# Splitting two feed-forward steps by head pair, and scoring two tiles in one task, in a planned attention and feed-forward kernel

## The chip, the cores and the metric

The kernel runs on one core of one Trainium2 chip. The metric is the device time of one execution in microseconds (us). Three runs of the kernel before gave 613.16, 611.17 and 612.41 us, so the median is 612.41 us. Names used below: PE is TensorE, PEld its weight loads, DVE is VectorE, ACT is ScalarE, POOL is GpSimd, SP is SyncE, whose queue issues nearly all DMAs.

## The reference

Attention over 4 batches, 8 heads, 768 positions of 64 features, in which a query sees the first 4 positions (sinks) and the last 128 positions up to itself; its output, as 3072 tokens of 512 features, goes through a feed-forward layer of width 2048 with an ELU.

```python
scores = scale * q @ k.T                    # scale = 1/8
keep = is_sink | ((rel >= 0) & (rel < window))
a = softmax(where(keep, scores, -1e9))      # per head
x = (a @ v) as [3072, 512]
h = x @ w_in                                # 512 -> 2048
g = where(h > 0, h, exp(min(h, 0)) - 1)
out = g @ w_out                             # 2048 -> 512
```

## The kernel before

**Tiles and chunks.** The 24 query tiles of 128 tokens are cut into nine chunks (CHUNKS). Chunks 0 and 1 hold two tiles each, all of them first tiles of a batch, whose scores are 128 columns wide. Chunk 2 holds two second tiles (260 columns), the others three tiles. Each chunk goes through four head pairs, then through sixteen feed-forward steps f of 128 hidden features; chunks 0 and 1 interleave theirs (PARTS): steps 0 to 6 of chunk 0, 0 to 12 of chunk 1, then the rest of each.

**Attention of one tile and pair, in chunks 0 and 1.** PE makes the scores of both heads from the f32 tile `kqs` (a ring of two, loaded by SP, L568) into banks `s0` and `s1` (L668). DVE adds the mask and takes the row minimum (L683), ACT takes the exponential and its sum (L688), ACT or POOL (L692) and DVE (L697) make the reciprocal. Chunk 0 then turns the result on PE: POOL scales an identity (L704, `pq`), PE multiplies (L710, into `acc`), ACT or DVE copies out (L714, `pt`), and PE multiplies by the values (L727, into `po`). From chunk 1 on ACT and DVE split the result into two f16 parts (L742, L743), SP transposes by DMA (L761), and PE multiplies by f16 parts of the values (L775). At the end of a pair ACT and DVE write the f16 parts of x (L817, L818).

**A feed-forward step.** PE makes h from the x of all four pairs and one weight piece in twelve products (L845), ACT the exponential (L854), POOL or DVE and then DVE the ELU (L856, L857), ACT and POOL its two f16 parts (L859, L866), and PE adds six or more products into `acc` (L873). h has two banks, so step f + 2 waits for L857 of step f. Each of the 32 weight pieces is loaded by SP (L354, `raw`) and unpacked by ACT (L347), DVE (L348), ACT (L507, high part) and POOL (L508, low part in two halves).

**What sets the order.** All of this is written as tasks with an assumed duration, their dependences and rings of buffers. A planner (class Plan) lays them out in time once, and every engine's instructions are issued in that order; an engine never passes a waiting instruction. For PE, `pos` gives a task's place within its line (scores, values, transposes, feed-forward are four lines), and a line's tasks are never swapped. SHIFTS holds seeds of random shifts of due times that the plan went through. Where the plan has a gap on PE in its first 100 us, `with_idle_products` puts in unread products of 240 columns of constants (L446), filling the share IDLE_FILL of it: 0.65, or 0.75 in the first 8 us.

Of the kernel before, what the change touches and what calls it, by code (L numbers as in the profile page):

```python
# [21 lines left out]
P = 128  # L22
B, H, S, D = 4, 8, 768, 64
# [3 lines left out]
ND = DM // P  # L27
# [3 lines left out]
KW = NS + P  # L31
# [18 lines left out]
ROUNDS = 8  # L50
SHIFTS = [600047, 600054, 600066, 600067, 600150, 600157, 600163, 600185, 600194, 600295, 600400, 600467, 600483, 600849, 601310, 601684, 602239, 602260, 603167, 603862]
VISIT = 2
PAIRS = 3
LATE = 1.0
SPARE = 0.1
KEEP = 1
DUP = 3
# [4 lines left out]
FIRST, IDLE_US, IDLE_UNTIL, IDLE_LEAST, IDLE_OVER, IDLE_WANT = (13, 2), 0.11, 100.0, 0.3, 3.4, 0.85  # L62
IDLE_FILL, IDLE_FIRST = (0.65, 0.75), 8.0
V_AT = 7
V_AT0 = 5.0
T_AT = 3.5
PE_T, PE_V = 0.25, 0.13
# [45 lines left out]
class Plan:  # L113
# [7 lines left out]
    def add(self, eng, dur, fn, *args, deps=(), lat=0.0, pos=None, or_=None, line=0, slow=1.0, lock=True):  # L121

        t = Task(eng, dur, fn, args, deps, lat, pos, slow)
        t.line = line
        t.lock = lock
        if or_:
            t.ways[or_[0]] = or_[1:]
        self.tasks.append(t)
        return t

    def ring(self, name, writers, users):

        r = self.rings.setdefault(name, [])
        r.append((writers, users))
# [268 lines left out]
def fast_path(tc, ctx, first, kq, vx, wt, out, low, spread, copied, numbers, flag):  # L403

    nc = tc.nc
# [30 lines left out]
    w = rows("w", [P, 2, 512], F16, NW)  # L436
# [29 lines left out]
    add, ring = plan.add, plan.ring  # L466
# [50 lines left out]
    base, pos = {}, 0  # L517
# [29 lines left out]
    def attention(c):  # L547
# [80 lines left out]
        for p in range(NP):  # L628
# [6 lines left out]
            for g in ts:  # L635
# [34 lines left out]

                if c >= DUP:
                    scs = [add("PE", 0.222 if nb == 2 else 0.2, scores([e]), deps=kqp[e][2:4], pos=at[k] + 0.01 * e, line=1) for e in range(2)]
                else:
                    scs = [add("PE", 0.7 if nb == 2 else 0.45, scores([0, 1]), deps=kqp[0][2:4], pos=at[k], line=1)] * 2
                for kk, sc_ in zip(kqp, scs):
                    kk[4].append(sc_)
                if c < DUP and j == 0:
# [3 lines left out]
                for e in range(2):  # L681
                    ee, me = e3[:, e, :wd], mn[:, e : e + 1]
                    red = add("DVE", 0.08 + 0.00103 * wd, lambda ee=ee, me=me, sp=sps[e], m=m, wd=wd, to_score=to_score: nc.vector.tensor_tensor_reduce(ee, sp[:, :wd], m[:, :wd], to_score, 3.0e38, ALU.add, ALU.min, me), deps=[scs[e], (None, second_)[t] if t < 2 else rest_])  # L683
                    ring(f"s{banks_of[e]}", [scs[e]], [red])
# [140 lines left out]
    def feed_forward(c, f0, f1, start):  # L825
# [7 lines left out]
        for f in range(f0, f1):  # L833
# [13 lines left out]

            s1 = add("PE", 12 * (n / 2400 + 0.002), stage1, deps=[v for d in x for v in d[2:4]] + list(w_done[2 * f]), pos=start + 2 * (f - f0))
            for d in x:
                d[4].append(s1)  # L850

# [5 lines left out]
            b = last_g[0] = add("DVE", dve_us(n), lambda gf=gf, hp=hp: nc.vector.scalar_tensor_tensor(gf, gf, 0.0, hp[:, :n], ALU.min, ALU.max), deps=[b])  # L857
            ring("h", [s1], [b])
            th = add("ACT", act_us(n), lambda gf=gf, gh=gh: nc.scalar.activation(gh[:, :n], gf, AF.Copy), deps=[b])  # L859
# [425 lines left out]
```

## Time and profile before

| | |
|---|---|
| median of three runs | 612.41 us |
| the profiled execution's own time | 615.44 us |
| its span, first to last instruction | 613.6 us |
| PE busy | 605.5 us (99%) |
| DVE, ACT, POOL busy | 480.7, 428.8, 307.2 us |
| last product of the last feed-forward step ends | near 608.7 us |
| first product of a feed-forward step (chunk 0) | 31.70 us |
| first product of chunk 1's feed-forward | 56.44 us |

The span is 1.84 us shorter than the profiled execution's own time. PE busy includes unread products, so a busy PE is no proof of useful work in the first 56 us. Instruction times in the rows overlap their neighbours by about a tenth of a microsecond, since an instruction starts before the one ahead of it has drained.

### The profile page before, as it was taken

To read this page: it belongs to the slowest core of one execution; us is meant where nothing else is said; L and a number is where in the kernel's file an instruction comes from. 1 tells how busy PE (TensorE), PEld (TensorE's weight loads), DVE (VectorE), ACT (ScalarE), POOL (GpSimd) and SP (SyncE) were. 2 spreads that over 40 slices of the span, in tenths; PEclk is the share of its full clock that TensorE was granted. 3 is DMA by queue.
4 is the path that set the end of the run, shared out by engine and by line. 5 is a ranking of instruction groups with operands and counts; after the bars stand their busy time and mean duration, and the time that the engine had idled before them with its cause. 6 is when DMAs were issued, how large, how long until landed. Compare 5 with 4: busy or idle time off the path is not lost.

```text
span 613.6 us, 13574 instructions
## 1 busy us (share of the span) xinstructions
PE 605.5 (99%) x4590; PEld 368.9 (60%) x4590; DVE 480.7 (78%) x1211; ACT 428.8 (70%) x1202; POOL 307.2 (50%) x587
## 2 busy tenths in 40 slices
PE   9899999999999999999999999999999999999996
PEld 6665666667765555656565565655656565556663
DVE  5798989799898568899799988799988977543333
ACT  6899999789888567786677766677766766422222
POOL 4766899646555343353454554345554544222221
PEclk9799999999999999999999999999999999999999
DMA  8899987879797545596678945699774893524201
GB/s 295 282 252 246 336 235 247 188 171 198 170 170 204 107 98 105 153 262 138 151 174 251 232 129 142 135 256 217 147 185 102 226 165 73 110 75 109 62 1 56
DMA packets 125999, 105.22 MB, mean 171 GB/s; under 512 B 100580, under 2 KB 100836, under 8 KB 125924
## 3 DMA queue, kind: packets, MB, share of 16 engines
q1 hardware_dynamic: 125780, 104.17, 67.9%
q8 instruction: 37, 0.61, 0.4%
q14 instruction: 38, 0.31, 0.2%
q10 hardware_dynamic: 144, 0.13, 0.1%
HBM read 72.82 MB, written 7.34 MB: 131 GB/s over the span
## 4 chain that ended last, share of the span: by engine, by line
PE 96%; DVE 1%; DMA 1%; issue 0%; ACT 0%
PE h L845 41%; PE acc L873 40%; PE po L775 3%; PE s L662 3%; PE s L663 3%; PE s L775 2%; PE s L668 2%; PE acc L446 1%; DMA kqs<-in_kq_dram 1%; PE po L873 1%; PE acc L710 0%; DVE wv L348 0%; PE s L780 0%; PE po L780 0%; DVE e L683 0%
## 5 line engine op out<-in xcount | busy, mean ns | idle before, releaser
L845 PE MATMUL h<-x,w 128*128 128x384 f16 (+1 forms) x1728 | 273.6, 308 | 0.0
L845 PEld LDWEIGHTS <-w 128*128 128x128 f16 x1728 | 168.3, 98 | 84.2 <-ACT g L854 0.3
L866 POOL TENSOR_TENSOR gl<-g,gh 128x384 f16<-128x384 f32 (+1 forms) x144 | 129.5, 900 | 140.6 <-ACT gh L859 132.4
L873 PE MATMUL acc<-w,gh 128*128 128x512 f16 (+1 forms) x768 | 190.3, 375 | 0.0
L873 PEld LDWEIGHTS <-gh 128*128 128x128 f16 x800 | 76.9, 98 | 65.5 <-ACT g L854 1.4
L854 ACT ACTIVATE g<-h 128x384 f32<-128x384 f32 (+1 forms) x144 | 64.6, 449 | 67.6 <-PE h L845 65.2
L688 ACT ACTIVATE e<-e,st 128x260 f32<-128x260 f32 (+1 forms) x192 | 93.1, 485 | 26.6 <-DVE st L683 24.4
L743 DVE SCALAR_TENSOR_TENSOR pq<-e,st,pq 128x256 f16<-128x256 f32 (+1 forms) x176 | 100.0, 588 | 14.6 <-ACT pq L742 13.9
L873 PE MATMUL acc<-w,gl 128*128 128x512 f16 (+1 forms) x384 | 107.8, 375 | 0.0
L859 ACT ACTIVATE gh<-g 128x384 f16<-128x384 f32 (+1 forms) x144 | 69.3, 482 | 54.0 <-DVE g L857 53.4
L683 DVE CUSTOM_DVE_ANT_0 e<-s,m 128x260 f32<-128x260 f32 (+1 forms) x192 | 75.4, 398 | 22.6 <-PE s L663 18.3
L742 ACT ACTIVATE pq<-e,st 128x256 f16<-128x256 f32 (+1 forms) x176 | 79.5, 488 | 13.1 <-DVE st L697 12.5
L857 DVE SCALAR_TENSOR_TENSOR g<-g,h 128x384 f32<-128x384 f32 (+1 forms) x144 | 72.3, 503 | 13.0 <-POOL g L856 11.7
L856 POOL TENSOR_SCALAR g<-g 128x384 f32<-128x384 f32 (+1 forms) x77 | 41.5, 539 | 64.2 <-ACT g L854 63.4
L856 DVE TENSOR_SCALAR g<-g 128x384 f32<-128x384 f32 (+1 forms) x67 | 27.8, 415 | 50.8 <-ACT g L854 50.1
L873 PEld LDWEIGHTS <-gl 128*128 128x128 f16 x400 | 39.1, 98 | 44.2 <-POOL gl L866 0.5
L577 ACT ACTIVATE kq<-kqs 128x912 f16<-128x912 f32 (+1 forms) x48 | 48.5, 1010 | 8.6 <-PE s L663 6.0
L508 POOL TENSOR_TENSOR w<-wv,w 128x256 f16<-128x256 f32 x64 | 52.4, 838 | 3.0 <-ACT w L507 2.3
L692 POOL TENSOR_SCALAR st<-st 128x2 f32<-128x2 f32 x83 | 24.7, 298 | 48.4 <-ACT e L688 43.3
L578 DVE SCALAR_TENSOR_TENSOR kq<-kqs,kq 128x528 f16<-128x528 f32 (+1 forms) x48 | 39.3, 818 | 2.6 <-ACT kq L577 2.1
L662 PE MATMUL s<-kq 128*128 128x260 f16 x144 | 39.5, 275 | 0.0
L663 PE MATMUL s<-kq 128*128 128x260 f16 x144 | 39.5, 274 | 0.0
(105 smaller groups left out, 676.9 us busy)
## 6 DMA issues: line engine op xcount, KB each, us to landing
raw<-in_wt_dram SPq DMA_DIRECT2D x32, 512.0 KB, 5.2
kqs<-in_kq_dram SPq DMA_DIRECT2D x24, 522.0 KB, 3.9
kqs<-in_kq_dram SPq DMA_DIRECT2D x24, 456.0 KB, 3.9
vs<-in_vx_dram SPq DMA_DIRECT2D x34, 256.0 KB, 3.5
vm<-in_kq_dram SPq DMA_DIRECT2D x24, 261.0 KB, 4.2
out_dram<-wv SPq DMA_DIRECT2D x23, 256.0 KB, 2.5
vm<-in_kq_dram SPq DMA_DIRECT2D x24, 228.0 KB, 4.2
vm<-in_vx_dram SPq DMA_DIRECT2D x9, 512.0 KB, 5.1
```

Source lines behind the costliest of these rows:

```text
L662: nc.tensor.matmul(sp[:, :wd], q, hi[:, c0 : c0 + wd], start=True, stop=False)
L683: red = add("DVE", 0.08 + 0.00103 * wd, lambda ee=ee, me=me, sp=sps[e], m=m, wd=wd, to_score=to_score: nc.vector.tensor_tensor_reduce(ee, ...
L688: ex = add("ACT", 0.278 + 0.00083 * wd, lambda ee=ee, me=me, rs=rs[:, e : e + 1]: nc.scalar.activation(ee, ee, AF.Exp, bias=me, scale=-1.0 ...
L742: a = add("ACT", act_us(nb * P, True), lambda src=src, hi=hi, re=re: nc.scalar.activation(hi, src, AF.Copy, scale=re), deps=[rr])
L743: b = add("DVE", 0.45 if nb == 2 else 0.3, lambda src=src, hi=hi, lo=lo, re=re: nc.vector.scalar_tensor_tensor(lo, src, re, hi, ALU.mult, ...
L845: nc.tensor.matmul(hp[:, :n], win[:, part, d, :], xx[:, :n], start=k == 0, stop=k == 3 * ND - 1)
L854: a = add("ACT", 0.13 + 0.00091 * n, lambda gf=gf, hp=hp, sums=sums: nc.scalar.activation(gf, hp[:, :n], AF.Exp, scale=1.0 / G_SCALE, accu ...
L856: b = add("DVE", 0.06 + 0.00057 * n, lambda gf=gf: nc.vector.tensor_scalar(gf, gf, -1.0, G_SCALE, ALU.add, ALU.mult), deps=[a], slow=2.1, ...
L857: b = last_g[0] = add("DVE", dve_us(n), lambda gf=gf, hp=hp: nc.vector.scalar_tensor_tensor(gf, gf, 0.0, hp[:, :n], ALU.min, ALU.max), dep ...
L859: th = add("ACT", act_us(n), lambda gf=gf, gh=gh: nc.scalar.activation(gh[:, :n], gf, AF.Copy), deps=[b])
L866: tls.append(add("POOL", pool_us(cut), lambda gl=gl, gf=gf, gh=gh, cut=cut: nc.gpsimd.tensor_tensor(gl[:, :cut], gf[:, :cut], gh[:, :cut], ...
L873: nc.tensor.matmul(bank[:, cs], gg[:, i * P : (i + 1) * P], wout[:, part, cs], start=f == f0 and k == 0, stop=f == f1 - 1 and k == 2)
```

## The change

Four edits act together, and all of them change only the first part of the program in what is computed when; the seeds are new, so the plan of the whole program is another one.

1. TWIN: in chunks 0 and 1 the scores of both tiles of a pair are one PE task of four products, with tile j in columns 128 j of the two score banks. The banks are free for the next pair when all four DVE reductions are done.
2. SPLIT: steps 0 and 1 of chunk 0 make h in four pieces of three products, one for each head pair, each depending on that pair's x and the weight piece alone. The last piece keeps the old place.
3. IDLE_FILL: unread products fill 0.85 of a planned gap in place of 0.65 (0.75 in the first 8 us as before). The program has 94 of them, before 75.
4. SHIFTS: 34 other seeds in place of 20.

```diff
-SHIFTS = [600047, 600054, ...
+SHIFTS = [1010003, 1010007, ...
+SPLIT = 2
+TWIN = (0,1,)
-IDLE_FILL, IDLE_FIRST = (0.65, 0.75), 8.0
+IDLE_FILL, IDLE_FIRST = (0.85, 0.75), 8.0
+SPLIT_AT = -8.0
...
+                if c in TWIN:
+                    sps = [s_ps[e][:, j * P : (j + 1) * P] for e in range(2)]
+                    if j == 0:
+                        def scores_of_all(qo=qo, c0=c0, kqp=kqp):
+                            for i in range(nt):
+                                for e in range(2):
+                                    r = slice(e * D, (e + 1) * D)
+                                    nc.tensor.matmul(s_ps[e][:, i * P : (i + 1) * P], ...)
+                        scs = [add("PE", 0.23 * nt + 0.2, scores_of_all, deps=kqp[0][2:4], pos=at[k], line=1)] * 2
+                        taken = [[], []]
+                        for e in range(2):
+                            ring(f"s{e}", scs[:1], taken[e])
...
+            def of_one(d, hp=hp, f=f):
+                win = w[2 * f].rearrange("p t (a f) -> p t a f", a=ND)
+                xh, xl = x[d][:2]
+                for k, (part, xx) in enumerate(((0, xh), (1, xh), (0, xl))):
+                    nc.tensor.matmul(hp[:, :n], win[:, part, d, :], xx[:, :n], ...)
+            if c == 0 and f < SPLIT:
+                ahead = [add("PE", 3 * (n / 2400 + 0.002), of_one, d, deps=list(x[d][2:4]) + list(w_done[2 * f]), pos=...) for d in range(ND)]
```

Line numbers move by 3 to 33. The places of the lines named here in the changed program: scores L682 (128 columns) and L671 (260), pieces of h L873, whole h L866, transposes L731, values L748, unread products L449, loads of kqs L571, of vs L595, of weight pieces L357, second products L906.

**SP's queue, the first loads.** `kqs_63` and `kqs_64` are the two buffers of the kqs ring, so their loads in turn are pairs 2 and 3 of chunk 0, then pairs 0 and 1 of chunk 1; `raw` is a weight piece, `vs_66` the values of the second tile. Before:

```order
L592 DMA vs_66<-in_vx_dram 128x512
L354 DMA raw<-in_wt_dram 128x2048 x4
L568 DMA kqs_63<-in_kq_dram 128x520
L354 DMA raw<-in_wt_dram 128x2048
L568 DMA kqs_64<-in_kq_dram 128x520
L354 DMA raw<-in_wt_dram 128x2048 x3
L568 DMA kqs_63<-in_kq_dram 128x520
L354 DMA raw<-in_wt_dram 128x2048 x2
L568 DMA kqs_64<-in_kq_dram 128x520
```

and in the changed program:

```order
L357 DMA raw<-in_wt_dram 128x2048
L595 DMA vs_66<-in_vx_dram 128x512
L357 DMA raw<-in_wt_dram 128x2048
L571 DMA kqs_63<-in_kq_dram 128x520
L357 DMA raw<-in_wt_dram 128x2048 x3
L571 DMA kqs_64<-in_kq_dram 128x520
L357 DMA raw<-in_wt_dram 128x2048
L571 DMA kqs_63<-in_kq_dram 128x520
L357 DMA raw<-in_wt_dram 128x2048
L571 DMA kqs_64<-in_kq_dram 128x520
```

The first pair of chunk 1 now has six weight pieces ahead of it (before eight), the second seven (before ten), and the first weight piece goes ahead of vs_66.

**PE's queue, from the third tile's transposes of chunk 0 on.** `acc` is written by transposes, `po` by values, `s` by scores, `h_165` is the h bank of step 0 and `w_133` its weights. Before:

```order
L710 MATMUL acc_169<-pq_108,e_99 128x128 x2
L727 MATMUL po_172<-pt_110,vs_66 64x128 x2
...
L710 MATMUL acc_170<-pq_106,e_97 128x128 x2
...
L727 MATMUL po_172<-pt_111,vs_65 64x128 x2
L668 MATMUL s_167<-kqs_63 128x128
L668 MATMUL s_168<-kqs_63 128x128
L727 MATMUL po_172<-pt_112,vs_66 64x128 x2
```

and in the changed program:

```order
L731 MATMUL acc_169<-pq_108,e_99 128x128 x2
L682 MATMUL s_167<-kqs_63 128x128
L682 MATMUL s_168<-kqs_63 128x128
...
L748 MATMUL po_172<-pt_111,vs_65 64x128 x2
L873 LDWEIGHTS w_133
L873 MATMUL h_165<-x,w_133 128x256
...
L731 MATMUL acc_170<-pq_106,e_97 128x128 x2
...
L748 MATMUL po_172<-pt_112,vs_66 64x128 x2
```

The scores of pair 2 (`kqs_63`, both tiles) went ahead of the last transposes of pair 1, and the first piece of step 0 now stands ahead of those transposes too.

**PE's queue, at the first product of chunk 1's feed-forward** (`h_166<-x,w_133`). `s<-kqs 128x260` are scores of chunk 2, `pt_112,vh_80` the last values of chunk 1. Before:

```order
L668 MATMUL s_167<-kqs_64 128x260
L668 MATMUL s_168<-kqs_64 128x260
L845 LDWEIGHTS w_133
L845 MATMUL h_166<-x,w_133 128x256
```

and in the changed program:

```order
L796 MATMUL po_172<-pt_112,vh_80 64x128
L671 MATMUL s_167<-kqs_63 128x260
L671 MATMUL s_168<-kqs_63 128x260
L449 LDWEIGHTS const-bfloat16-1.0
L449 MATMUL acc_171<-const-bfloat16-1.0 128x240
L866 LDWEIGHTS w_133
L866 MATMUL h_166<-x,w_133 128x256
```

Before, four score tasks of chunk 2 stand ahead of this product (the last one of kqs_64); now there are five (the last one is the next pair's, kqs_63). All else that stands ahead of it, unread products aside, is equal in number: 84 products of h, 30 second products, and the scores, transposes and values of chunks 0 and 1.

## Rows read from the trace of the kernel before

**Rows 1.** Busy us by engine and stage, granted TensorE clock (PEclk), DMA.

```profile
core 0: us, PE busy (x) PEld busy (x) DVE busy (x) ACT busy (x) POOL busy (x), PEclk, DMA share, GB/s
24.00:32.00 8.00, 7.95 (x48) 6.04 (x49) 5.12 (x21) 6.26 (x20) 5.24 (x7) 0.60 0.87 309
32.00:56.40 24.40, 23.94 (x202) 14.98 (x200) 21.58 (x77) 24.40 (x89) 18.83 (x34) 1.00 0.94 218
56.40:608.70 552.30, 552.28 (x4208) 333.46 (x4207) 437.83 (x1045) 380.00 (x1040) 268.73 (x510) 1.00 0.67 163
```

**Rows 2.** The chain that ended last, 0 to 64 us: start, us, what.

```profile
17.16 0.71 PE s L668 x3
17.88 6.03 DMA kqs<-in_kq_dram
24.05 0.80 PE s L668 x4
24.85 2.00 PE acc L710 x8
26.85 0.62 PE po L727 x4
28.92 0.87 PE acc L710 x4
31.86 1.31 PE h L845 x12
56.51 1.42 PE h L845 x12
```

**Rows 3.** ACT in order of time: start, us, what [idle before <-releaser].

```profile
5.67 0.40 ACT L688 ACTIVATE e<-e,st 128x128 f32<-128x128 f32 x1 [3.33 <-DVE st L683]
26.76 0.40 ACT L688 ACTIVATE e<-e,st 128x128 f32<-128x128 f32 x1 [1.19 <-DVE st L697]
30.86 0.38 ACT L817 ACTIVATE x<-po 128x256 f16<-128x256 f32 x1 [0.28 <-PE po L727]
55.62 0.36 ACT L817 ACTIVATE x<-po 128x256 f16<-128x256 f32 x1
```

**Rows 4.** ACT by line, 0 to 56.4 us: count, busy us, mean ns, idle before.

```profile
L688 ACT ACTIVATE e<-e,st 128x128 f32<-128x128 f32 (+1 forms) x36 | 14.5, 404 | 5.9 <-DVE st L683 4.7 <-DVE st L697 1.2
L347 ACT ACTIVATE wu<-raw 128x512 f16<-128x512 bf16 x14 | 10.8, 770 | 0.0
L507 ACT ACTIVATE w<-wv 128x512 f16<-128x512 f32 x14 | 8.6, 621 | 0.7 <-DVE wv L348 0.7
L742 ACT ACTIVATE pq<-e,st 128x128 f16<-128x128 f32 (+1 forms) x17 | 6.0, 398 | 0.0
L817 ACT ACTIVATE x<-po 128x256 f16<-128x256 f32 x8 | 2.9, 368 | 0.5 <-PE po L727 0.5
```

**Rows 5.** PE in order of time, as rows 3.

```profile
4.38 0.80 PE L668 MATMUL s<-kqs 64*128 64x128 f32 x4
10.52 0.71 PE L710 MATMUL acc<-pq,e 128*128 128x128 f32 x4
15.43 0.49 PE L668 MATMUL s<-kqs 64*128 64x128 f32 x4
24.05 0.80 PE L668 MATMUL s<-kqs 64*128 64x128 f32 x4 [0.66 <-DMA kqs<-in_kq_dram]
35.36 1.48 PE L845 MATMUL h<-x,w 128*128 128x256 f16 x12
48.48 0.71 PE L668 MATMUL s<-kqs 64*128 64x260 f32 x4
53.04 0.59 PE L446 MATMUL acc<-const-bfloat16-1.0 128*128 128x240 bf16 x4
```

**Rows 6.** SP's queue, 0 to 70 us: waited for, us in total, times, longest.

```profile
SPq L568 <- PE s L668: 12.0, 5, 4.3
```

**Rows 7.** POOL in order of time, as rows 3: low halves of the first weight pieces.

```profile
13.46 1.75 POOL L508 TENSOR_TENSOR w<-wv,w 128x256 f16<-128x256 f32 x2
15.53 4.28 POOL L508 TENSOR_TENSOR w<-wv,w 128x256 f16<-128x256 f32 x5 [0.32 <-ACT w L507]
```

More of the change, by code (lines that the diff above doesn't have):

```diff
@@ L50 @@
 ROUNDS = 8
-SHIFTS = [600047, 600054, 600066, 600067, 600150, 600157, 600163, 600185, 600194, 600295, 600400, 600467, 600483, 600849, 601310, 601684, 602239, 602260, 603167, 603862]
+SHIFTS = [1010003, 1010007, 1010026, 1010053, 1010059, 1010083, 1010114, 1010156, 1010214, 1010335, 1010370, 1010388, 1010446, 1010468, 1010520, 1010534, 1010619, 1010737, 1010767, 1010772, 1010927, 1011110, 1011137, 1011191, 1011408, 1011660, 1012947, 1012951, 1013013, 1013279, 1013732, 1013934, 1013984, 1014001]
 VISIT = 2
+SPLIT = 2
+TWIN = (0,1,)
 PAIRS = 3
@@ L669, in scores @@
                     return run
-                if c >= DUP:
+                if c in TWIN:
[5 more added lines that the diff above has]
+                                    r = slice(e * D, (e + 1) * D)
+                                    nc.tensor.matmul(s_ps[e][:, i * P : (i + 1) * P], kqp[0][0][r, qo + i * P : qo + (i + 1) * P], kqp[0][0][r, c0 + i * KW : c0 + i * KW + P], start=True, stop=True)
+                        scs = [add("PE", 0.23 * nt + 0.2, scores_of_all, deps=kqp[0][2:4], pos=at[k], line=1)] * 2
+                        taken = [[], []]
+                        for e in range(2):
+                            ring(f"s{e}", scs[:1], taken[e])
+                elif c >= DUP:
                     scs = [add("PE", 0.222 if nb == 2 else 0.2, scores([e]), deps=kqp[e][2:4], pos=at[k] + 0.01 * e, line=1) for e in range(2)]
@@ L675, in attention @@
                 for kk, sc_ in zip(kqp, scs):
-                    kk[4].append(sc_)
+                    if c not in TWIN or j == 0:
+                        kk[4].append(sc_)
                 if c < DUP and j == 0:
@@ L683, in attention @@
                     red = add("DVE", 0.08 + 0.00103 * wd, lambda ee=ee, me=me, sp=sps[e], m=m, wd=wd, to_score=to_score: nc.vector.tensor_tensor_reduce(ee, sp[:, :wd], m[:, :wd], to_score, 3.0e38, ALU.add, ALU.min, me), deps=[scs[e], (None, second_)[t] if t < 2 else rest_])
-                    ring(f"s{banks_of[e]}", [scs[e]], [red])
+                    if c in TWIN:
+                        taken[e].append(red)
+                    else:
+                        ring(f"s{banks_of[e]}", [scs[e]], [red])
                     red.spare = SPARE if c >= PAIRS else 0.0
@@ L846, in stage1 @@
                         k += 1
-            s1 = add("PE", 12 * (n / 2400 + 0.002), stage1, deps=[v for d in x for v in d[2:4]] + list(w_done[2 * f]), pos=start + 2 * (f - f0))
-            for d in x:
-                d[4].append(s1)
+            def of_one(d, hp=hp, f=f):
+                win = w[2 * f].rearrange("p t (a f) -> p t a f", a=ND)
+                xh, xl = x[d][:2]
+                for k, (part, xx) in enumerate(((0, xh), (1, xh), (0, xl))):
+                    nc.tensor.matmul(hp[:, :n], win[:, part, d, :], xx[:, :n], start=d + k == 0, stop=d == ND - 1 and k == 2)
+            if c == 0 and f < SPLIT:
+                ahead = [add("PE", 3 * (n / 2400 + 0.002), of_one, d, deps=list(x[d][2:4]) + list(w_done[2 * f]), pos=start + 2 * f if d == ND - 1 else SPLIT_AT + 2.4 * d + 0.01 * f) for d in range(ND)]
+                for d, s1 in zip(x, ahead):
+                    d[4].append(s1)
+                h_first = ahead[0]
+            else:
+                h_first = s1 = add("PE", 12 * (n / 2400 + 0.002), stage1, deps=[v for d in x for v in d[2:4]] + list(w_done[2 * f]), pos=start + 2 * (f - f0))
+                for d in x:
+                    d[4].append(s1)
             at = (c * NF + f + 1) % nc1
@@ L857, in feed_forward @@
             b = last_g[0] = add("DVE", dve_us(n), lambda gf=gf, hp=hp: nc.vector.scalar_tensor_tensor(gf, gf, 0.0, hp[:, :n], ALU.min, ALU.max), deps=[b])
-            ring("h", [s1], [b])
+            ring("h", [h_first], [b])
             th = add("ACT", act_us(n), lambda gf=gf, gh=gh: nc.scalar.activation(gh[:, :n], gf, AF.Copy), deps=[b])
```

## The prediction

> **What bounds the kernel now.** I read the busy times by stage first, then the chain of waits, then PE's and ACT's instructions in order of time, and last what SP's queue waits for. The stages show that from 56.4 to 608.7 us PE is busy for 552.28 of 552.30 us [rows 1]; the span ends 4.9 us later. Nothing in that stretch waits on PE, so the end is fixed by two things: when the first product of chunk 1's feed-forward starts (56.44, on the chain at 56.51 [rows 2]), and how much PE work is still behind it. What the change does before that point counts only as far as it moves these two.
>
> In the 24.4 us before it ACT is busy for 24.40 us, PE for 23.94 [rows 1]. Both look full, but the product at 56.51 needs the x of chunk 1's last pair, which ACT starts to write at 55.62 [rows 3]; until then ACT has no idle time since 30.86. So ACT decides: the end of the stage is the time at which ACT comes to that instruction, which is its work ahead of it plus its idle time since its first exponential at 5.67 [rows 3]. That idle time is 5.9 - 3.33 = 2.6 us ahead of exponentials, 0.7 ahead of L507 and 0.5 ahead of L817, 3.8 us in all [rows 3, 4], and it lies before 31 us. The largest single gap, 1.19 us, ends at 26.76 [rows 3]. The chain says where it comes from: the scores at 17.16 release a kqs buffer, its load takes from 17.88 to 23.9, PE waits 0.66 us for it at 24.05, and two tiles' transposes stand behind these scores in PE's queue [rows 2, 5]. From there the granted clock is low (0.60 in the mean of 24 to 32 us [rows 1], so mostly the level of 1.2 GHz).
>
> **The change part by part.**
>
> *Scores of two tiles in one task.* The number of products is the same. It moves the second tile's scores up to the first's. SP waited 12.0 us in five waits for scores before it could issue a load of kqs [rows 6]; these waits shrink. For the load at 17.88: the first tile's scores of that pair ended near 15.9 (15.43 + 0.49), the second tile's would end 0.4 later, near 16.3, so the load starts at least 1.5 us earlier and, with the same 6.03 us, lands near 22.4, ahead of 24.05. That the order puts two fewer weight pieces ahead of it is not counted. The 0.66 us wait goes. The cost: DVE's first reduction now reads the bank that is written last, so it waits for four products in place of two: 0.73 us later at the start, where four rows take 0.80 less their overlap [rows 5]. This is idle time of ACT at its first exponential; it is in the sum below as a part of what ACT does not win.
>
> *Clock after 24 us.* The chain's pieces there are long: scores 0.80 where the same take 0.49 at 15.43, eight transposes 2.00 where two groups of four take 0.71 each, four more transposes 0.87 against 0.71 [rows 2, 5]. That is 0.31 + 0.58 + 0.16, about 1.1 us, with the values' 0.62 perhaps 1.3. In the changed order PE has 24 products of h and more unread products in that stretch and no wait for a load, so I take it at the full level. Together: 0.66 + 1.1 = 1.8 us for ACT's x of chunk 0's last pair (30.86) at the least. The most is ACT's whole idle time less the later start, 3.8 - 0.7 = 3.1. I take 2.3, nearer to the end that rests on rows.
>
> *ACT's own queue.* Counting the two orders up to that x: the changed one has two L347 and two L507 fewer ahead of it (1.54 + 1.24 us), two L742, one exponential with its sum and one L714 more; net about 1.3 us less. Up to the x of chunk 1's last pair the two orders differ by 0.1 us of work only. So 1.3 us of weight work that before was done ahead of 30.86 now stands between the two, in the stage where ACT has no gap: 2.3 - 1.3 = 1.0 us is left. The x comes at 54.6 in place of 55.62. Bounds: no gain at all if ACT's gaps only move (0), and 3.1 - 0.1 = 3.0 us.
>
> *Steps 0 and 1 by head pair.* 24 products of 256 columns, 2.6 us at 1.31 for twelve [rows 2], move into PE's early gaps; 18 of them stand ahead of the last x. This frees PE by up to 2.6 us at step 2 (35.36 [rows 5]). I cost it at nothing in the sum: what is late next is step 0's exponential and ELU (step 2 needs its bank), and then ACT's x of chunk 1; PE would only wait there. If PE were the bound, the 2.6 us would count in full.
>
> *Unread products.* 19 more, at about 0.13 us by the four that take 0.59 at 53.04 [rows 5]. Groups of 14 now stand before step 2 of chunk 0 and between two score tasks of chunk 2. They lie where PE waits for ACT and cost nothing; without that cover a group of 14 costs up to 1.8 us.
>
> *One more score task of chunk 2 ahead of the point that counts.* Five in place of four, by the order; one row of it takes 0.71 less an overlap [rows 5], 0.65 us. This work is taken out of the stretch without gaps and done where PE waits for ACT. That is a gain of 0.65 whatever else happens, unless its load is late.
>
> *The rest of the plan.* After the point the kinds of work and their neighbours on PE are the same in number, so the 552.3 us stay, less the 0.65.
>
> Sum: 1.0 + 0.65 = 1.65 us off the span of 613.6, so 611.95; the profiled execution's own 615.44 would be 613.8. The runs shown have a median of 612.41, 3.0 below that execution; I put the same difference on them: 610.8 us.
>
> **The rivals.**
>
> *B, PE's lead survives.* ACT's gaps all go and the new order feeds it without a break. Then the x comes 3.0 us earlier, and with 0.65 the time is 612.41 - 3.65 = 608.8. For it: the kqs loads come up to several us earlier, and 3.8 us of idle are there to be had. Against it: ACT starts 0.7 later, and 4.7 - 3.33 = 1.4 us of its idle time come from DVE's reductions [rows 4], which now wait for more products than before.
>
> *C, slower: the pieces of step 0 and 1 block PE's queue.* The first piece stands ahead of the transposes of pair 1's second tile, and the pieces of step 1 ahead of pair 3's scores. Each needs a whole weight piece. Before, POOL ended the first one's low halves at 15.2 and the second one's near 17.2 [rows 7], and PE needed neither until 31.86 [rows 2]. If POOL is not earlier, PE waits about 1.7 us twice, everything of chunk 0 behind it is 3.4 us late, and the slow clock stays as it was: the gain of 2.3 is not made, the x of chunk 1 comes at 55.62 + 3.4 + 0.1, the time is 612.41 + 3.5 - 0.65 = 615.3. It decides once the two waits together exceed about 2 us. For it: POOL's first halves now stand behind three scaled identities. Against it: SP loads the first weight piece before vs_66 now, and before, PE came to that place with unread products to spare. The Trainium skill, "TensorE: Matmul & The Clock Gate", Part 2, step-by-step, says that matmuls stay in program order and only weight loads are pulled ahead; by that rule any late weight is paid by all transposes behind it, as in this rival. The trace agrees: at 24.05 PE waited 0.66 us for a load with eight transposes behind it [rows 5].
>
> *D, nothing comes through.* ACT's gaps move but stay, and the fifth score task waits for its load, which in the order stands behind one of the transposes of chunk 1's last pair. Then the point is at 56.4 as before and the time between 611.8 and 613.0. For it: every us of this stage was ACT's already.
>
> **How the numbers follow.** Forecast 0.52, with 609.9 to 611.9 as its own range; B 0.16; C 0.12; D 0.20. A difference of 0.3% is 1.84 us, about what a measurement of this kernel can tell from none. Below 610.57 lie B and half of the forecast's case: 0.16 + 0.26 = 0.42 for faster. The other half and D give 0.46 for the same, C gives 0.12 for slower. The range from 608.8 to 613.0 leaves out most of C and the far end of B.
>
> **What would show it.** Right: no wait for kqs near 24 us and a granted clock of 1.00 from about 10 us on; the load of chunk 1's first pair issued by 16.5; x of chunk 0's last pair near 28.6 on ACT and of chunk 1's near 54.6; PE waiting or in unread products for one to two us ahead of that; 551.6 us without a gap behind it. Wrong: any PE wait after 60 us (then the new seeds, not the early edits, set the time); PE waiting for w before 18 us (C); the first product of chunk 1 at 53.5 or earlier (B).

## The result and the profile after

The changed kernel takes 615.61 us (median of 8 runs, 614.79 to 618.75), the kernel before 611.96 (8 runs, 611.17 to 613.19): a ratio of 1.0053, 95% interval 1.0035 to 1.0072. Timed again beside 26 runs of the kernel before it took 615.09 against 612.11, a ratio of 1.0039 (1.0021 to 1.0057). So the change costs 2.4 to 3.2 us by the two ratios. Forecast were 610.8 us, with a range up to 613.0: the sign is wrong, and the time is outside the range.

The profiled execution took 615.83 us with a span of 613.9. Its busy times by stage (as [rows 1]; the stages are cut at ACT's x of the last pair of chunk 0 and of chunk 1, and at the first product of chunk 1's feed-forward):

```profile
core 0: us, PE busy (x) PEld busy (x) DVE busy (x) ACT busy (x) POOL busy (x), PEclk, DMA share, GB/s
0.00:29.61 29.61, 25.57 (x190) 18.32 (x190) 19.86 (x94) 21.20 (x71) 17.00 (x43) 0.88 0.78 261
29.61:56.66 27.05, 24.54 (x216) 16.18 (x213) 24.95 (x80) 26.20 (x90) 19.82 (x33) 1.00 1.09 265
57.31:609.00 551.69, 551.66 (x4204) 333.12 (x4202) 432.57 (x1038) 381.75 (x1044) 270.40 (x510) 1.00 0.68 162
```

The third row is as forecast: PE has no gap, and the stretch is 0.6 us shorter than the 552.3 of [rows 1]. All that is lost is lost ahead of it. In the second row ACT is busy for 26.20 of 27.05 us, where the kernel before needed 24.76 for the same stage (30.86 to 55.62 in [rows 3]). ACT's gaps in order of time, and the two x:

```profile
5.47 0.40 ACT L709 ACTIVATE e<-e,st 128x128 f32<-128x128 f32 x1 [3.12 <-DVE st L701]
9.33 0.40 ACT L709 ACTIVATE e<-e,st 128x128 f32<-128x128 f32 x1 [1.98 <-DVE st L701]
11.82 0.39 ACT L735 ACTIVATE pt<-acc 128x256 f32<-128x256 f32 x1 [0.89 <-PE acc L731]
29.61 0.36 ACT L838 ACTIVATE x<-po 128x256 f16<-128x256 f32 x1
56.66 0.38 ACT L838 ACTIVATE x<-po 128x256 f16<-128x256 f32 x1 [0.65 <-PE po L796]
```

The gap at 9.33 stands where the first profile of before had two shorter ones, 0.61 and 0.73 us at 7.39 and 9.24; the one at 11.82 is new, and so is the one at 56.66, in a stage where ACT had none [rows 3]. What PE waited for, in us, times and longest:

```profile
PE s L682 <- DMA kqs<-in_kq_dram: 2.0, 1, 2.0
PE po L796 <- DMA pt<-pq: 1.0, 1, 1.0
PE s L671 <- DVE st L701: 1.0, 2, 0.6
```

and PE at these places:

```profile
7.77 1.23 PE L682 MATMUL s<-kqs 64*128 64x128 f32 x8 [1.99 <-DMA kqs<-in_kq_dram]
56.27 0.25 PE L796 MATMUL po<-pt,vh 128*64 128x128 f16 x2 [1.03 <-DMA pt<-pq]
57.31 1.47 PE L866 MATMUL h<-x,w 128*128 128x256 f16 x12
```

The wait of 0.66 us at 24.05 [rows 5] is gone, as forecast. In its place PE comes to the twin scores of pair 1 at 5.8 us, 1.99 us before their load lands, with the transposes of pair 0 behind them. The last values of chunk 1 wait 1.03 us for a DMA transpose. SP's queue from 9 to 29 us (start, us until its issues of one kind are through):

```profile
9.03 0.33 SPq L571 DMA_DIRECT2D kqs<-in_kq_dram  x1
9.40 0.44 SPq L357 DMA_DIRECT2D raw<-in_wt_dram  x1
15.66 0.33 SPq L571 DMA_DIRECT2D kqs<-in_kq_dram  x1
18.18 0.33 SPq L357 DMA_DIRECT2D raw<-in_wt_dram  x1
19.89 0.33 SPq L571 DMA_DIRECT2D kqs<-in_kq_dram  x1
20.27 4.07 SPq L357 DMA_DIRECT2D raw<-in_wt_dram  x2
24.44 0.38 SPq L571 DMA_DIRECT2D kqs<-in_kq_dram  x1
24.87 0.42 SPq L357 DMA_DIRECT2D raw<-in_wt_dram  x1
```

From 9.84 to 15.66 SP issues nothing: the reload of kqs at the head of its queue waits for the next twin scores (4.1 us) and for a load of kqs (1.7), with weight pieces behind it. The DMA engines are full in that time. It is behind it, up to 26 us, that they are idle in part (the last but one number of a row is their share):

```profile
9.80:15.70 5.90, 5.90 (x38) 4.23 (x38) 3.91 (x19) 4.24 (x14) 2.98 (x6) 0.64 1.00 399
15.70:26.00 10.30, 9.38 (x82) 6.57 (x83) 9.03 (x36) 9.44 (x35) 7.80 (x12) 1.00 0.66 191
```

There SP waits longest for DVE ahead of weight pieces, and 1.3 us for scores:

```profile
SPq L357 <- DVE st L718: 3.6, 1, 3.6
SPq L357 <- DVE wv L351: 2.1, 1, 2.1
```

What was issued up to the x of chunk 0's last pair (count, KB each, median us to landing):

```profile
raw<-in_wt_dram SPq DMA_DIRECT2D x10, 512.0 KB, 6.7
kqs<-in_kq_dram SPq DMA_DIRECT2D x8, 260.0 KB, 4.4
```

The same view of the kernel before has 13 weight pieces in a stretch 1.25 us longer (30.86). The three missing pieces go out among chunk 1's transposes, whose time from issue to landing (minimum, median, maximum, 0 to 62 us) was 2.7/3.1/4.9 us before, and is now:

```profile
DMA to landing us min/median/max: 3.3/5.7/7.6
```

### The profile page after: what moved, and what is told of

Read it like the earlier page. It is cut to its first block, busy times and chain, and to the rows that moved or that the text cites. A ratio compares the mean times of both kernels' runs of the same rounds, so it can differ in the third digit from the quotient of the medians.

```text
span 613.9 us, 13611 instructions
## 1 busy us (share of the span) xinstructions
PE 602.5 (98%) x4609; PEld 367.9 (60%) x4609; DVE 477.6 (78%) x1210; ACT 430.2 (70%) x1205; POOL 307.2 (50%) x585
## 4 chain that ended last, share of the span: by engine, by line
PE 91%; DMA 3%; ACT 3%; DVE 2%; issue 1%; SPq 0%; POOL 0%; ACTq 0%
PE h L866 39%; PE acc L906 39%; PE po L796 3%; PE s L665 3%; PE s L666 3%; PE s L796 2%; DMA pt<-pq 2%; DMA kqs<-in_kq_dram 1%; ACT e L709 1%; PE po L906 1%; DVE wv L351 1%; ACT wu L350 0%; PE acc L449 0%; PE s L671 0%; ACT w L510 0%
## 5 line engine op out<-in xcount | busy, mean ns | idle before, releaser
L866 PE MATMUL h<-x,w 128*128 128x384 f16 (+1 forms) x1704 | 270.7, 309 | 0.5 <-DVE g L890 0.5
L866 PEld LDWEIGHTS <-w 128*128 128x128 f16 x1704 | 166.0, 98 | 83.8 <-issue 1.0
L906 PE MATMUL acc<-w,gh 128*128 128x512 f16 (+1 forms) x768 | 190.3, 375 | 0.0
L906 PEld LDWEIGHTS <-gh 128*128 128x128 f16 x800 | 77.0, 98 | 64.9 <-issue 0.3
L906 PE MATMUL acc<-w,gl 128*128 128x512 f16 (+1 forms) x384 | 107.8, 375 | 0.0
L889 POOL TENSOR_SCALAR g<-g 128x384 f32<-128x384 f32 (+1 forms) x77 | 43.3, 562 | 72.3 <-ACT g L887 71.3
L889 DVE TENSOR_SCALAR g<-g 128x384 f32<-128x384 f32 (+1 forms) x67 | 29.9, 446 | 51.3 <-ACT g L887 50.7
L906 PEld LDWEIGHTS <-gl 128*128 128x128 f16 x400 | 39.1, 98 | 44.2 <-POOL gl L899 0.5
L581 DVE SCALAR_TENSOR_TENSOR kq<-kqs,kq 128x528 f16<-128x528 f32 (+1 forms) x48 | 41.5, 864 | 3.4 <-ACT kq L580 3.2
L713 POOL TENSOR_SCALAR st<-st 128x2 f32<-128x2 f32 x81 | 21.7, 268 | 42.7 <-ACT e L709 34.6
```

Source lines behind the costliest of these rows:

```text
L866: nc.tensor.matmul(hp[:, :n], win[:, part, d, :], xx[:, :n], start=k == 0, stop=k == 3 * ND - 1)
L889: b = add("DVE", 0.06 + 0.00057 * n, lambda gf=gf: nc.vector.tensor_scalar(gf, gf, -1.0, G_SCALE, ALU.add, ALU.mult), deps=[a], slow=2.1, ...
L906: nc.tensor.matmul(bank[:, cs], gg[:, i * P : (i + 1) * P], wout[:, part, cs], start=f == f0 and k == 0, stop=f == f1 - 1 and k == 2)
```

## The experiments

In all kernels but two (e1 and e6) the planner's order is that of its base, and the edit is made on the finished order. "Before" is the kernel before in the same session.

| run | base and edit | us | before | ratio (95%) |
|---|---|---|---|---|
| e0 | before, again | 612.85 | 612.95 | 1.0004 (0.9984 to 1.0024) |
| e10 | before, fill 0.85 | 612.81 | 612.83 | 1.0004 (0.9994 to 1.0014) |
| e21 | before, first loads swapped | 612.45 | 612.11 | 0.9997 (0.9979 to 1.0015) |
| e19 | before, ACT 1.26 us more | 614.55 | 612.11 | 1.0033 (1.0018 to 1.0047) |
| e18 | before, kqs loads ahead of weights | 616.87 | 612.80 | 1.0073 (1.0047 to 1.0099) |
| e6 | before, new seeds | 623.88 | 612.83 | 1.0194 (1.0175 to 1.0213) |
| e20 | changed, again | 615.09 | 612.11 | 1.0039 (1.0021 to 1.0057) |
| e1 | changed, no twin | 626.27 | 612.95 | 1.0223 (1.0195 to 1.0250) |
| e13 | changed, pieces together | 615.51 | 612.99 | 1.0046 (1.0028 to 1.0064) |
| e3 | changed, fill 0.65 | 614.71 | 612.83 | 1.0040 (1.0026 to 1.0055) |
| e5 | changed, early gap filled | 616.15 | 612.95 | 1.0064 (1.0039 to 1.0089) |
| e8 | changed, first loads as before | 615.58 | 612.83 | 1.0050 (1.0034 to 1.0066) |
| e11 | changed, pair 1's keys first | 614.95 | 612.99 | 1.0037 (1.0018 to 1.0057) |
| e12 | e11, nine products out | 615.18 | 612.99 | 1.0031 (1.0015 to 1.0047) |
| e14 | e12, fill 0.65 | 615.90 | 612.99 | 1.0058 (1.0037 to 1.0078) |
| e4 | changed, two loads later | 615.47 | 612.95 | 1.0063 (1.0043 to 1.0084) |
| e15 | changed, five loads ahead | 615.42 | 612.80 | 1.0045 (1.0023 to 1.0067) |
| e16 | e15 with e11 | 615.00 | 612.80 | 1.0044 (1.0025 to 1.0062) |

**e0, e10: was the profile of before typical?** e0 is the kernel before without an edit.

> The kernel before, unchanged, once more. Open: its one profiled execution took 615.4 us where its eight timed ones have a median of 612.0. Theory P (that profile is not typical): another profile has a span near 610, no stretch at half clock after 20 us, and the first product of chunk 1's feed-forward near 53 to 54 in place of 56.4. Rival Q (a profile always costs about 3 us): the span is again near 613.5 and that product near 56.4. Time against before: 612 by both.

> The kernel before with one difference: 0.85 of each early gap of PE is filled with unread products in place of 0.65 (10 products more, all in the first 40 us; the rest of the order is untouched). Theory P (the time of the kernel before varies from 611.4 to 616 with the stretch at the granted clock's lower level between 20 and 30 us; in the best executions there is none): the stretch goes, and the median falls from 612.9 to 611.4. Theory N (the clock of that stretch is of no account to the end): 612.9 as before.

```diff
-IDLE_FILL, IDLE_FIRST = (0.65, 0.75), 8.0
+IDLE_FILL, IDLE_FIRST = (0.85, 0.75), 8.0
```

It was not. In e0's profile the x of chunk 0's last pair stands at 28.18 and the first product of chunk 1 at 53.53, against 30.86 and 56.44. Its stages, cut at the two x:

```profile
0.00:28.18 28.18, 25.63 (x178) 17.87 (x179) 20.82 (x88) 22.58 (x71) 19.64 (x44) 0.94 0.86 311
28.18:52.79 24.61, 23.90 (x204) 15.14 (x201) 21.67 (x79) 24.61 (x92) 18.64 (x33) 1.00 1.00 218
```

e10, with ten unread products more, has no stretch at the lower level at all:

```profile
core 0: us, PE busy (x) PEld busy (x) DVE busy (x) ACT busy (x) POOL busy (x), PEclk, DMA share, GB/s
0.00:27.39 27.39, 25.11 (x187) 17.57 (x188) 20.71 (x88) 22.23 (x70) 19.06 (x43) 1.00 0.90 323
27.39:52.33 24.94, 24.28 (x206) 15.24 (x205) 21.61 (x79) 24.70 (x92) 18.94 (x34) 1.00 0.95 220
```

Its x are at 27.39 and 52.33, its span is 610.3. But its median is that of the kernel before: what the prediction wanted to win at that place was not in the median to begin with. The mean granted clock of each run says the same. Of 118 runs of the kernel before (e0's 12 and those timed beside the experiments) 105 have 0.998 or more, with a median of 612.42 us; the four at 0.994, which is the first profile's clock, took 615.63 to 616.08. Theory P holds for the profile, not for the 1.5 us that it promised e10.

**e13, e3: the split and the unread products.**

> The changed kernel with the split undone at the chip alone: the four pieces of step 0 stand together where its last piece stood, and so do those of step 1; the order of all else, the unread products too, is the same. The prediction costed the split at nothing (ACT decides); its rival C had the pieces block PE's queue for 3.4 us. If the split is worth nothing: 615.6. If the pieces were in the way of transposes and scores (they wait for x and w with ACT's work behind them): 613.5 to 615. If they do what PE lacks time for later: the 18 products that were done early come back in front of step 2, 2 us, 617.5.

```diff
+    for f in range(SPLIT):
+        group = ...            # the four pieces of step f
+        move group[:-1] to the place just ahead of group[-1]
```

> The changed kernel with 0.65 of each early gap filled in place of 0.85; all tasks in the same order, fewer unread products. The prediction had these products at nothing. Theory U (they cost: groups of 14 stand ahead of work that is ready): 614 or less. Theory Z (they cost nothing): 615.6, or up to 1 us more if the granted clock falls for longer than with them.

e3 is e10's edit the other way, in the changed kernel. Neither ratio can be told from the changed kernel's 1.0053 and 1.0039. With intervals of about 1 us to either side, the split and these products neither cost nor bring more than some 1.5 us; that they are worth nothing is not shown.

**e1, e6: the parts planned anew.**

> The changed kernel without the joint scores (TWIN empty); split steps, fill and seeds as in the change; the plan is made anew. Theory T: with the loads of kqs back behind the second tile's scores, weight loads come earlier and fewer of them (6, not 8) fall between 32 and 57 us; transposes land in 3 to 4 us and the time is 612 to 613. Rival N (the new seeds, a worse plan, cost the time): still 615 to 616.

> The kernel before, planned with the seeds of the changed kernel; nothing else. It tells what another order of the same tasks is worth without scores in twos, without pieces of steps and without more unread products. Theory N (the order that the new seeds bring costs the 3 us, whatever stands in it): 615 to 616. Theory L or S (the order of the changed kernel is late because of what the edits put into it): 612 to 613.5, or another value that has nothing to do with 615.6, since seeds that were drawn for other tasks fit these only by accident.

```diff
-TWIN = (0,1,)
+TWIN = ()
```

e6 has the line SHIFTS of the changed kernel in the kernel before. Both are some 11 us slower than their bases, which no theory had for e1. Seeds drawn for one set of tasks are worth that much less for another, so a part that is undone by planning anew says nothing on the part, and the cost of the new seeds' order stays untested. All others therefore keep the order.

**e5, e8, e11, e12, e14: the early wait.**

> The changed kernel with 13 more unread products ahead of the scores of pair 1, where PE waited 1.99 us for a kqs load at 5.8 us and the granted clock was low until 13.9. Theory G (this wait and the low clock behind it cost the start): with the wait filled the clock stays at full after 8 us, the x of chunk 0's last pair comes 1 to 2 us earlier than 29.6, and the time falls to 613.6 to 614.6. Theory T: chunk 0 may come earlier, but chunk 1's feed-forward still starts when its last transposes land, so the time stays at 615.6 within 0.7, with PE waiting longer for them.

> The changed kernel with one difference: the first seven loads on SP's queue stand in the order that they had before the change (values of tile 6, weight pieces 0, 2, 1, 4, the second kqs buffer's reload, piece 3). In the changed order SP issues piece 0 ahead of the values and then waits 1.3 us for the scores of pair 0 with pieces 1 and 4 behind it; the DMA share of 0 to 29.6 us is 0.78 there against 0.86 in the kernel before. Theory L (the early loads cost ACT its work: pieces come late, pair 1's keys come late, ACT stands idle for 8.4 us ahead of the x of chunk 0's last pair against 5.6): no PE wait near 7.7, ACT's idle time there 1.5 to 2.5 us less, time 613 to 614. Theory S (what counts is the 1.6 us of weight work that now lies in the stage between the two chunks, and the seeds' plan behind it): the early waits change, the time stays at 615 to 616.

> The changed kernel with one difference: the load of pair 1's keys and queries (kqs) is issued ahead of the load of tile 0's values at the start, so 0.47 us earlier and with one load less beside it. In four profiles of the changed order PE waits 1.2 to 2.0 us for this load at about 7.1 to 7.8 us, ACT has then waited 1.0 to 2.0 us for an exponential at 8.3 to 9.3 and 0.9 us for the first transposed tile after it; the kernel before has no such gaps, and ACT's idle time ahead of the x of chunk 1's last pair is 5.4 us there (best profile) against 7.1 to 9.3. Theory K (the twin scores of pair 1 are reached before their load, and this early gap is what the change costs): the wait shrinks by about 1 us, the x of chunk 1's last pair and the time are 1 us earlier, 614.5. Theory S (the weight work in the stage between the chunks costs it): the early wait shrinks, 615.5.

```diff
-            ("vs", 0, vx, 0, VT),
             ("kqs", 1, kq, KQ_OFF[0, 2], nk * KW + qc),
+            ("vs", 0, vx, 0, VT),
```

> As the run with pair 1's keys first, and besides the 9 unread products that stand between the scores of pair 1 and the transposes of pair 0 are taken out; the rest of the order is the same. They took 1.9 us in the profile, with the transposes, which ACT then waits for, right behind. Theory K: ACT's 0.9 us ahead of L735 goes too, the time is 2 us below the changed kernel's, 613.5. Theory S: 615.5. If the granted clock then stands at half for a while: no gain, or 1 us worse.

> As the run before this one (keys first, no nine products), with 0.65 of the gaps filled in place of 0.85. The run with 0.65 alone had 614.7. Theory K: the gains add, 612.5 to 613, as fast as the kernel before and not faster, since 1.3 to 1.6 us of weight work still stands in the stage between. Theory S: 614.5.

e11 does to chunk 0 what theory K said, and more: no gap of ACT at 9.33 and 11.82, the x of chunk 0's last pair at 26.78. But then ACT has new gaps:

```profile
26.78 0.36 ACT L854 ACTIVATE x<-po 128x256 f16<-128x256 f32 x1
29.59 0.63 ACT L616 ACTIVATE vh<-vs 128x512 f16<-128x512 f32 x1 [1.09 <-DMA vs<-in_vx_dram]
55.32 0.38 ACT L854 ACTIVATE x<-po 128x256 f16<-128x256 f32 x1 [1.28 <-PE po L812]
```

Of 2.8 us that chunk 0 gains, 1.3 are left at 55.32, and none in this execution's span of 614.3. A load of values and the transposes now come last. In e5, e8 and e12 the gap of 1.98 us at 9.33 shrinks to 0.96, 0.95 and 0.77, in e14 it is gone, and ACT's x of chunk 1's last pair comes at 54.43, 55.55, 55.66 and 55.16, in place of 56.66; the medians do not follow. In e5 the stretch of low clock is gone too (1.00 in the mean up to 27.82), so theory G falls. K falls as the one cause: none of the five is below the changed kernel by more than its interval.

**e4, e15, e16: the loads taken out again.**

> The changed kernel with one thing moved: in SP's queue the loads of weight pieces 15 and 14 stand behind the last DMA transposes of chunk 1; no other engine's order changes. Theory T (in the changed kernel the transposes share the DMA engines with weight loads issued just ahead of them, and the last one, 5.7 us from issue to landing where before had 3.1, decides when chunk 1's feed-forward starts): the last transposes land about 2 us sooner, the first product of chunk 1 comes at 55 to 55.5 in place of 57.3, and the time falls to 613 to 614. Theory S (ACT's work decides, as predicted, and the transposes only happen to end with it): ACT writes that x within 0.5 us of where it did, and the time stays at 615.6 within 0.7. Theory G (the early wait and low clock decide): unchanged, 615.6.

> The changed kernel with one difference, on SP's queue alone: five loads of weight pieces (6, 8, 10, 11, 12) are issued ahead of the reloads of kqs behind which they stood, or of the first transposes, so that SP no longer waits for twin scores with free DMA engines. In the profiles of the changed order 10 weight pieces are issued before the x of chunk 0's last pair against 13 in the kernel before, the DMA engines are busy for 78 to 84% of that stretch against 90%, and 7.2 MB in place of 5.5 are moved between the two chunks' last x, with eight transposes among them. Theory Q (the order on SP's queue is the cost: pieces that come late lie among the transposes, and any gain ahead of them is given back there): 13 pieces early, DMA share 0.9, ACT's waits for values and for the last transposes in the stage go, time 613.5 to 614.5. Theory S (the 1.6 us of ACT work in that stage alone): the DMA changes, ACT's queue is as before, 615.5.

> The loads ahead as in the run before, and pair 1's keys first as in the run of that name. With the keys first alone the x of chunk 0's last pair came at 26.78, 2.8 us earlier than in the changed kernel, but 2.4 us of it were given back before chunk 1's (1.1 us waiting for a load of values, 1.3 us for transposes). Theory Q: nothing is given back now, x of chunk 1's last pair near 53.0, first product of chunk 1 near 53.7 (53.0 in the best profile of the kernel before), time 612.5 to 613.5, the kernel before's. Theory S: 614.9 as with the keys first alone.

```diff
+    put_after(raw 6, raw 5); put_after(kq (1, 0), raw 7); put_after(raw 8, kq (1, 0))
+    put_after(raw 10, wb 4); put_after(raw 11, wb 5); put_after(raw 12, wb 6)
```

(`wb k` is DVE's conversion of piece k; e4 moved pieces 14 and 15 behind chunk 1's last transpose.) In e15 12 weight pieces are out by the x of chunk 0's last pair, in place of 10, and ACT stands idle for 0.28 us between the two x; the second comes at 54.95, and the time is 615.42. Of the two pieces that now stand ahead of the reload at which SP stood still, one goes out at 11.99, the other only at 17.10, after 4.7 us of waiting for DVE. So the stop did not stand in the way of both, and the engines were not free in it, as the expectation has it. In e16 the first product of chunk 1 comes at 54.55, 2.8 us earlier than in the changed kernel. Then PE, which had no wait after 57 us, has some:

```profile
89.74 1.38 PE L882 MATMUL h<-x,w 128*128 128x256 f16 x11 [0.37 <-POOL w L513]
113.04 1.47 PE L882 MATMUL h<-x,w 128*128 128x256 f16 x12 [0.37 <-DVE g L906]
```

Theory Q's mechanism shows in chunk 1's start, its time does not: 615.0, not 612.5 to 613.5. In e4 the same: the wait for transposes is gone, and 1.3 us of waits for ACT and DVE stand between 60 and 69.

**e18, e19: the suspected costs put into the kernel before.**

> The kernel before with one difference, on SP's queue alone: the reloads of kqs for chunk 1's first three pairs are moved ahead of the weight pieces, as far as their buffers allow (after the second tile's scores), and four weight pieces (10 to 13) behind the first four transposes of chunk 1, about where the changed order has them. No scores in twos, no pieces of steps, the same unread products, the same order on every other engine. It adds the suspected cost to the kernel that doesn't have it. Theory Q: ACT waits for weight pieces and transposes land later in the stage, 614 to 616. Theory S (ACT's order, which stays): 613.

```diff
+    put_after(kq (1, 0), scores (0, 5)); put_after(kq (1, 2), scores (0, 7)); put_after(kq (1, 4), scores (1, 1))
+    put_after(raw 10, T 0); put_after(raw 11, T 1); put_after(raw 13, T 2); put_after(raw 12, T 3)
```

(`T j` is the j-th transpose of chunk 1, counted from 0.) The kernel before then loses 4.1 us by the medians, with nothing but loads moved. Chunk 0 ends as in e10, at 27.38; in the stage behind it ACT waits for weight pieces:

```profile
35.87 0.78 ACT L348 ACTIVATE wu<-raw 128x512 f16<-128x512 bf16 x1 [0.62 <-DMA raw<-in_wt_dram]
43.63 0.78 ACT L348 ACTIVATE wu<-raw 128x512 f16<-128x512 bf16 x1 [2.08 <-DMA raw<-in_wt_dram]
69.98 0.79 ACT L348 ACTIVATE wu<-raw 128x512 f16<-128x512 bf16 x1 [1.24 <-DMA raw<-in_wt_dram]
```

That is another loss than the changed kernel's: there ACT waits for a weight piece once in the first 130 us, for 0.5 us. So e18 shows what late pieces can cost, not that they are what the change costs.

> The kernel before with one difference: two of ACT's conversions of weight pieces (6 and 7, L507, ahead of the x of chunk 0's last pair) are done twice, with the same result; nothing else, and no load, is moved. It adds 2 x 0.63 = 1.26 us of work to ACT at about 20 to 25 us. Theory A (ACT, which is busy for 98.5 of the first 105 us in the best profile of the kernel before and for 95.2 in the changed one's, sets the end: time that it loses early is not won back): 614.0 to 614.2 against 612.9. Theory B (PE's lead hides it, or the loads set the pace): 612.9 to 613.2.

```diff
+    for k in (6, 7):           # the conversion L507 of these pieces is issued twice
+        v.fn = lambda fn=v.fn: (fn(), fn())
```

1.26 us of ACT's time cost 2.0 us by the ratio (1.1 to 2.9 by its interval): theory A. PE's lead hides little of it, if any.

**e20, e21: the changed kernel again, and a try to beat both.**

> The changed kernel itself once more, for a second profile and for its time beside the kernel before on the same chip. Its first profile had a stretch at the granted clock's lower level from 7 to 14 us, which none of six profiles of the same order with small differences had for as long. If that profile was typical: x of chunk 0's last pair near 29.6, first product of chunk 1 near 57.3. If not: near 27.8 and 55.0, as in the run with less fill. The time in either case 615 to 616.

> The kernel before with two swaps among its first loads: pair 1's kqs ahead of tile 0's values, and weight piece 0 ahead of tile 6's values (the second is how the changed kernel has it, the first what took away its early wait). In the best profile of the kernel before ACT waits 0.47 us for piece 0 at 9.42. Theory A (ACT's idle time counts in full): 0.3 to 0.5 us faster, 612.4, if the values are not late for it. Otherwise: 612.9 to 613.5.

e20's profile has the x of chunk 0's last pair at 28.67, in place of 29.61, but that of chunk 1's at 56.89:

```profile
9.34 0.40 ACT L709 ACTIVATE e<-e,st 128x128 f32<-128x128 f32 x1 [1.79 <-DVE st L701]
11.81 0.38 ACT L735 ACTIVATE pt<-acc 128x256 f32<-128x256 f32 x1 [0.88 <-PE acc L731]
31.20 0.63 ACT L608 ACTIVATE vh<-vs 128x512 f16<-128x512 f32 x1 [0.80 <-DMA vs<-in_vx_dram]
56.89 0.38 ACT L838 ACTIVATE x<-po 128x256 f16<-128x256 f32 x1 [1.26 <-PE po L796]
```

The gain of 0.9 us is given back at a load of values and at the transposes, as in e11. Its stages, cut at the two x:

```profile
0.00:28.67 28.67, 24.73 (x190) 17.96 (x190) 19.81 (x94) 21.03 (x70) 17.02 (x43) 0.94 0.80 269
28.67:56.89 28.22, 24.53 (x216) 16.17 (x213) 24.67 (x80) 26.16 (x90) 19.91 (x33) 1.00 1.08 254
```

e21 is no faster than the kernel before, and no kernel tried here is.

**The account of ACT's time.** In the first 105 us ACT is busy for 98.53 us in e10 and for 95.23 in the changed kernel:

```profile
0.00:105.00 105.00, 102.06 (x804) 67.42 (x805) 91.02 (x262) 98.53 (x302) 85.24 (x135) 1.00 0.92 278
```

```profile
0.00:105.00 105.00, 98.44 (x790) 66.67 (x790) 89.73 (x260) 95.23 (x293) 79.91 (x126) 0.97 0.94 273
```

The spans, 610.3 and 613.9, differ by 3.6 us, the busy times by 3.3. Span and busy time together give 708.8 and 709.1. In the other profiles of these two orders the sum is: before's first 709.6, e0 708.3, e21 709.0, e18 708.3, e19 708.6 (without its 1.26), e20 708.9, e13 709.3, e3 709.2, e5 709.1, e8 709.5, e11 709.4, e12 709.1, e14 709.0, e4 709.0, e15 709.1, e16 709.1. The spans go from 610.3 to 614.3, the sums from 708.3 to 709.6. So in these executions what ACT has not done by then comes on top at the end, wherever and why ever it stood idle. (e1 and e6, with plans of their own, have 713.2 and 715.1.) The sum tells executions apart, not medians: the profiled one of e5 took 613.96 us where e5's median is 616.15, that of e18 614.78 against 616.87. And it is an account, not a cause; that lost time of ACT counts is shown by e19, for the kernel before.

## Why the prediction was wrong

**The step that failed: "Together: 0.66 + 1.1 = 1.8 us for ACT's x of chunk 0's last pair (30.86) at the least"**, with the 2.3 us taken for it, and behind it "in the stage where ACT has no gap". The 2.3 us were to come out of ACT's idle time. Up to that x this idle time was 8.0 us in the first profile of before (30.86 - 22.84) and is 8.4 and 7.6 in the two profiles of the changed kernel. The x did come earlier, at 29.61 and 28.67, but because 1.6 and 1.8 us of ACT's work were put off behind it; that 28.67 is close to the 28.6 of the forecast is luck. In the stage behind it, forecast without a gap, ACT then stands idle for 0.85 and 2.06 us, and its last x, that of chunk 1's last pair, comes at 56.66 and 56.89 in place of 54.6.

The wait and the low clock that were to go belong to one execution of the kernel before: e0 has a shorter stretch, e10 none, and e10's median is unmoved. "I put the same difference on them" carried a gain to the median that the median didn't hold. Against e0 the last x of the changed kernel is 3.9 and 4.1 us late. ACT's work up to it is 47.19 us in e0 and 47.41 and 47.19 here, so nearly all of that is idle time: 2.8 and 2.0 us more of it ahead of the first x, 0.85 and 2.1 behind. The bound "no gain at all if ACT's gaps only move (0)" had no place for gaps that grow.

**Two terms that were misread.** The 0.31 us of the scores at 24.05 are not all the clock's: [rows 5] has four such products at 0.80 at 4.38 too, where the clock was at its full level. And the 0.73 us that DVE's first reduction was to come later did not show: ACT's first exponential is at 5.47 and 5.67, before at 5.67.

**Where the gaps grow.** One place is the twin itself: pair 1's scores were due before their load lands, 1.99 us of PE and 2.9 of ACT. The other is the stage between the two x, where a load of values or chunk 1's last transposes come late. The text had one thing of it in hand: "That the order puts two fewer weight pieces ahead of it is not counted". Three pieces fewer are out when chunk 0's last x is written, and more of them go out among the transposes. Scores hold up only some of them: SP's waits for scores did shrink, from 12.0 us [rows 6] to 8.2 in the same view (7.7 for L682, 0.5 for L671), and pieces wait for DVE as well (e15). That the late pieces are what the change costs is not shown: e18 loses as much by another wait, and e15, which sends them out earlier, is not faster than the changed kernel by more than its interval.

**The deferral was right**: 1.3 us of weight work between the two x was forecast. ACT's work there is 26.20 us, against 24.76 in the first profile of before and 24.61 in e0, so 1.4 to 1.6 more.

**What held.** ACT decides until chunk 1 starts, in the kernel before (e19); in the changed one its last x waits for a transpose besides. The stretch behind is gapless. One score task of chunk 2 ahead is worth about 0.65: from the first product of chunk 1 to the span's end it is 556.6 us after, 557.2 in the first profile of before. The split at nothing, and the unread products, within what e13 and e3 can tell.

**The rivals.** C had the sign and nearly the time, 615.3, by another mechanism: no piece waits for a weight, only once 0.5 us for x, and e13 is no faster. So its time is luck. D's "ACT's gaps move but stay" was nearest in kind, but ended at 613.0. None had gaps that grow.

**What stays open** is which edit brings the 3 us, and how they divide: e1 and e6 lie too far off to tell the twin from the order that the new seeds bring. Each of the two places, mended alone (e11, e15) or both (e16), leaves 2.3 to 2.8 us by the ratios. What is gained ahead of chunk 1's x is given back in part behind it: in e16's profile 2.8 us become 1.5 of the span. In e16 the loads go out earlier, but ACT and DVE still convert the pieces in the changed order. In every profile of that order ACT has 26.1 to 26.6 us of work between the two x, in those of the order before 24.6 to 24.8. An order of loads and conversions made together wasn't tried.

## What to carry to other kernels

Before a gain is taken from a stall in a profile, look at a second execution, or see whether the profiled one's own time is the median's: here it was 3 us above, and the stall was that execution's own. When a DMA queue stands still behind a load that waits, look whether the DMA engines stand still too, and whether the loads behind it were ready: here the engines were full until about 15 us, and of two pieces behind the load one could go at 12 us, the other not before 17 (e15). And where one engine is nearly full for a long time, add up its idle time over all of it: the account of ACT's first 105 us tells these executions apart better than any one wait.

## What the runs showed of the hardware

- The stretch in which TensorE's clock is granted at its lower level (1.2 GHz) moves between executions of one program: 23.6 to 30.4 us in the first profile of before, 22 to 25.5 in e0; in the changed kernel 7 to 14 in the first profile (0.52 there), shorter in e20 (8.2 to 11.5). PE had stood idle for 0.4 to 2 us at or ahead of its start each time. Such a wait does not always bring it: in e8 PE waited 1.12 us at 14.38, and the clock was 1.00 in the mean of the first 30 us.
- In e10's profile there is no such stretch, and its median is that of the kernel before (612.81 against 612.83). In single runs of the kernel before a low mean clock goes with a long time: 615.63 to 616.08 us at 0.994, a median of 612.42 at 0.998 and above.
- DMA transposes took longer from issue to landing where more 512 KB weight pieces were issued among the first eight of them: medians up to 62 us of 3.1, 2.8 and 3.8 us in three profiles of the order before (the first, e0, e10), with three pieces, and 5.7 and 4.8 in the two of the changed kernel, with six. That the pieces are the reason is not shown by these alone.
